# Phases rounded inside PSUM by matrix products, and new instruction orders for all engines of a two-layer spectral kernel

## The chip, the cores and the metric

The kernel runs on one core of a Trainium2 chip. The metric is device time in microseconds (us) of one execution. Five engines work side by side, each through its own queue in order: TensorE (PE, with its weight loads as PEld), VectorE (DVE), ScalarE (ACT), GpSimd (POOL) and SyncE (SP), which issues nearly all DMAs.

## The reference

Two kinds of layer alternate, A, B, A, B, each behind a layer norm and added to its input. A is a spectral filter (a 2-D FFT over 2048 rows and 512 channels, a product with weights, the way back); B is a diagonal state-space convolution (S4D): its kernel K of 2048 taps for each of the 512 channels is a sum over 128 complex powers, and the convolution runs through an FFT of length 4096.

```python
def _A_ref(x, w_r, w_i):
    X = rfft2(x, axes=(-2, -1)) * (w_r + 1j * w_i)
    return irfft2(X, s=(S, D), axes=(-2, -1))

def _B_ref(u, log_A_real, A_imag, C_real, C_imag, log_dt, D_skip):
    dt = jnp.exp(log_dt)
    A = -jnp.exp(log_A_real) + 1j * A_imag
    C = (C_real + 1j * C_imag) * dt[:, None]
    P = jnp.exp((A * dt[:, None])[:, :, None] * pos[None, None, :])
    K = 2.0 * jnp.einsum("dn,dnl->dl", C, P).real
    y = irfft(rfft(u_t, L2) * rfft(K, L2)[None], L2)[:, :, :L]
    return y.transpose(0, 2, 1) + u * D_skip[None, None, :]

x = x + _A_ref(_layernorm(x), A_w_r, A_w_i)
x = x + _B_ref(_layernorm(x), ...)
x = x + _A_ref(_layernorm(x), A_w_r, A_w_i)
x = x + _B_ref(_layernorm(x), ...)
```

Both B layers have the same K, which is made once.

## The kernel before

**FFTs as matrix products.** All transforms are products on TensorE in float32. A product of 128 output rows is issued as two products that take one half of the array's columns each (`halves`, L330), or as a list of products that lie side by side in the array (`side_by_side`, L336). Most take 128 rows of the array and 64 columns. The rows step of layer B (`p<-t,w` in the first, `p<-t,x` in the second B layer) takes 64 rows and 64 columns, four products at a time.

**K's time values.** `kernel_time` makes K in 32 units of 16 channels' states. For a unit, `grow` makes three tiles of magnitudes (`mag`): products of the constants `kb` with the states `th` in bfloat16, then exponentials on ScalarE. Each unit has two *turns*. `bend` makes the phases of a turn, counted in whole turns of the circle, in a PSUM tile `pk` by 4 products of 256 columns; VectorE rounds them to the nearest whole number by adding and subtracting 1.5 x 2^23 (`MAGIC`), into the bfloat16 tile `kw` (L864); two products of 512 columns with a negative identity `ni` subtract `kw` from `pk` again. What is left lies within half a turn. `sine` (an absolute value and a sine) and `cosine` run on ScalarE, `terms` multiplies both with the magnitudes on VectorE (L886, L888), `total` sums over the states on TensorE (`pv<-qp`, L899), ScalarE copies the sums to `stage` (L907), and a DMA takes them to the array `kt` in HBM. `kernel_freq` reads `kt` back and transforms it; layer B multiplies with the result (`kf`).

**What runs beside what.** K's 64 turns are interleaved with the first layer A and the beginning of the first layer B, since they need nothing of x. The last turn has to be done before the last block of K can be transformed.

**What sets the order.** After the program is built, `take_turns` lays the instructions of every engine in the order of the table `TURNS`: one string of places for each engine, found by a search outside the kernel. `ROOMS` says in the same way which buffer of a pool each tile takes, and `WARM` how many constant products are put ahead of which tile: `ps` issues them on a tile `warm` of ones into the PSUM tile that the next product overwrites. Nobody reads them; they keep TensorE from standing still.

## Time and profile before

| | us |
|---|---|
| median of 3 runs | 716.46 |
| lowest and highest | 710.45, 718.14 |
| span of the profiled execution | 713.4 |
| busy: PE, DVE, ACT, POOL | 626.0, 601.9, 438.2, 357.3 |
| products of the constant tile `warm`, part of PE's | 73.8 |
| mean granted TensorE clock | 0.973 |

The profile gives the profiled execution by its span, from the first to the last instruction; its own time beside that is not given apart, and the runs' median lies 3.1 us above the span. Busy times of one engine are unions: products that run side by side in the array count once. A float32 product leaves two records in the trace, a bfloat16 product one. Times in what follows are counted from the span's start.

### The profile page before, as it was taken

The numbers are of one execution on the slowest core, as the hardware profiler recorded it, in microseconds if no ns is written. First come the engines' busy times: TensorE is split into PE (matmuls) and PEld (weight loads), VectorE is DVE, ScalarE is ACT, GpSimd is POOL, SyncE is SP. The second block draws the span as 40 slices with busy tenths as digits, with TensorE's granted clock in tenths as the row PEclk, the third lists the DMA queues.
The fourth block names the chain that finished last, engine by engine and source line by source line (L and its number), as shares of the span: only waits on it lengthen the run. The fifth ranks groups of instructions, "written<-read, shape, count | busy, mean of one in ns | idle before, by whom it ended". The sixth has DMA issues, their size and how long they took to land. (4 is left out here: it accounts for less than half of the span.)

```text
span 713.4 us, 23503 instructions
## 1 busy us (share of the span) xinstructions
PE 626.0 (88%) x9580; PEld 491.3 (69%) x9580; DVE 601.9 (84%) x1348; ACT 438.2 (61%) x946; POOL 357.3 (50%) x565
## 2 busy tenths in 40 slices
PE   4459989989996999889999997984989899999996
PEld 3237867878674867667858876774877766577876
DVE  4998497998999799969999676869588699799993
ACT  3558999997664796778868524333767427333322
POOL 1533528672852704543196356452056484286870
PEclk9779999999999999999999999997999999999999
DMA  8602611613558350455544689222123103335514
GB/s 282 229 0 89 210 48 47 122 62 43 167 133 245 107 138 32 65 128 94 163 62 136 195 198 246 80 106 75 61 77 89 46 2 104 125 103 149 156 34 111
DMA packets 137355, 81.32 MB, mean 114 GB/s; under 512 B 70976, under 2 KB 116928, under 8 KB 136352
## 3 DMA queue, kind: packets, MB, share of 16 engines
q1 hardware_dynamic: 136992, 79.30, 40.1%
q8 instruction: 76, 1.25, 0.7%
q0 software_dynamic: 256, 0.52, 0.4%
q14 instruction: 31, 0.25, 0.1%
HBM read 54.90 MB, written 25.43 MB: 113 GB/s over the span
## 5 line engine op out<-in xcount | busy, mean ns | idle before, releaser
L1003 POOL TENSOR_TENSOR u<-wb,wb 64x512 f32<-64x512 f32 x90 | 123.2, 1373 | 66.0 <-DVE wb L991 60.9
L336 PE MATMUL p<-z,mb 128*64 128x512 f32 (+2 forms) x480 | 108.0, 517 | 1.7 <-DVE wb L991 1.3
L899 PE MATMUL pv<-qp 128*64 128x128 f32 x1024 | 81.6, 279 | 5.0 <-ACT stage L907 4.2
L991 DVE TENSOR_TENSOR wb<-p,kk 128x512 f32<-128x512 f32 x128 | 81.5, 676 | 4.3 <-POOL u L1003 2.3
L336 PEld LDWEIGHTS p<-mb,u 128*64 128x64 f32 x2048 | 73.1, 138 | 13.1 <-issue 6.7
L336 PE MATMUL p<-mb,u 128*64 128x64 f32 x2048 | 74.3, 223 | 4.4 <-issue 2.0
L663 ACT COPY z<-p 128x512 f32<-128x512 f32 x96 | 52.4, 595 | 41.8 <-PE p L336 31.6
L669 DVE STREAM_TRANSPOSE z<-z 128x512 f32<-128x512 f32 x96 | 59.3, 675 | 19.8 <-ACT z L663 19.7
L899 PEld LDWEIGHTS pv<-qp 128*64 128x64 f32 x1024 | 64.4, 139 | 15.8 <-ACT stage L907 6.9
L1113 POOL TENSOR_SCALAR w<-w,norms 128x128 f32<-128x128 f32 x64 | 34.7, 554 | 67.7 <-DMA w<-h 29.8
L547 POOL TENSOR_TENSOR w<-w,w 64x257 f32<-64x257 f32 x48 | 34.7, 724 | 66.8 <-DVE w L542 45.3
L1015 ACT COPY u<-p 128x512 f32<-128x512 f32 x64 | 35.9, 590 | 48.7 <-PE p L336 45.3
L330 PE MATMUL p<-w,w 128*64 128x256 f32 x256 | 38.2, 438 | 27.8 <-DVE w L463 11.6
L330 PE MATMUL pk<-kb,th 96*64 96x256 bf16 (+1 forms) x384 | 56.5, 312 | 1.5 <-DVE qp L888 1.1
L542 DVE TENSOR_TENSOR w<-wt,p 128x514 f32<-128x514 f32 x64 | 42.7, 688 | 17.1 <-PE p L336 9.6
L864 DVE TENSOR_SCALAR kw<-pk 128x512 bf16<-128x512 f32 x64 | 42.9, 680 | 16.5 <-PE pk L330 16.1
L330 PE MATMUL p<-warm 128*64 128x128 f32 x612 | 49.2, 284 | 3.2 <-DVE half L1139 1.1
L336 PE MATMUL p<-t,w 64*64 64x128 f32 x1024 | 42.1, 280 | 10.2 <-DMA w<-kt 3.5
L336 PEld LDWEIGHTS p<-z,mb 128*64 128x64 f32 x480 | 39.7, 137 | 16.1 <-issue 7.9
L330 PEld LDWEIGHTS p<-w,w 128*64 128x64 f32 x256 | 24.7, 156 | 36.3 <-DVE w L463 12.7
L336 PE MATMUL p<-w,ca 128*64 128x257 f32 x256 | 45.0, 385 | 4.1 <-ACT w L526 1.5
L832 ACT ACTIVATE kf<-pk 128x512 f32<-128x512 f32 x64 | 38.8, 606 | 15.4 <-PE pk L330 13.8
(179 smaller groups left out, 1617.1 us busy)
## 6 DMA issues: line engine op xcount, KB each, us to landing
wt<-in_w SPq DMA_DIRECT2D x32, 257.0 KB, 2.7
kf<-kk SPq DMA_DIRECT2D x32, 256.0 KB, 3.3
kk<-kf SPq DMA_DIRECT2D x32, 256.0 KB, 2.7
u<-in_x SPq DMA_DIRECT2D x16, 256.0 KB, 6.8
hr<-in_x SPq DMA_DIRECT2D x16, 256.0 KB, 3.9
kt<-stage SPq DMA_DIRECT2D x32, 128.0 KB, 5.2
h<-hr SPq DMA_DIRECT2D x16, 256.0 KB, 3.0
w<-kt SPq DMA_DIRECT2D x32, 128.0 KB, 3.1
```

What stands on the lines that cost most here:

```text
L330: self.nc.tensor.matmul(out[64 * r:64 * r + 64], weights[:, 64 * r:64 * r + 64], data, **k)
L336: last = self.nc.tensor.matmul(out, weights, data, start=not more, stop=True, skip_group_check=True).ins
L542: nc.vector.tensor_mul(m[pl], W, px[:, None, :].to_broadcast([128, 2, 257]))
L547: e[0].tensor_sub(Y[0:64, v], m[0][hs, 0], m[1][hs, 1])
L663: nc.scalar.copy(tiles["z"][:, :, :, b, m:m + 2].rearrange("p u j m r -> p (u j) (m r)"), ps[b].rearrange("p u j m r -> p (u j) (m r)"))
L669: nc.vector.transpose(tiles["zt"][:, u:u + 8].rearrange("p u j d -> p (u j d)"), tiles["z"][:, u:u + 8].rearrange("p u j b m r -> p (u j b ...
L832: nc.scalar.activation(*a, **k)
L864: nc.vector.tensor_scalar(whole, p, MAGIC, -MAGIC, op0=ALU.add, op1=ALU.add)
L899: nc.tensor.matmul(p[64 * t:64 * t + 64, g], QP[:, c, 2, d:d + 2].rearrange("p s a -> p (s a)"), QP[:, c, 0:2, d:d + 2].rearrange("p k s b ...
L991: nc.vector.tensor_mul(split(m[c, pl], "du", [32, 16]), by_channel(p), split(k[c], "du", [32, 16]))
L1003: self.added = e[0].tensor_sub(y[0:64], v[0, 0], v[1, 1]), e[1].tensor_add(y[64:128], v[0, 1], v[1, 0])
L1015: nc.scalar.copy(V[:, :, j, :, d:d + 8].rearrange("p n q d -> p q n d"), p.rearrange("p (q n) d -> p q n d", q=2))
```

## The change

Three edits go together.

The rounding moves to TensorE. `bend` now adds 1.5 x 2^23 to `pk` by a product of a bfloat16 tile `big`, which holds that number everywhere, with a weight tile that has a single row of ones (the first half of `ni`), and subtracts it by a second one with a row of minus ones; the sum in PSUM is then the rounded phase. Four more products of 256 columns subtract the phases from it again, with the negative constants LQ and LP at the end of `kb`. The sign of what is left turns over, so the sine's scale does too. The tile `kw` goes.

All orders (`TURNS`) and buffers (`ROOMS`) are new; `phase` lays out the rooms of its pools before any is used, and some tiles of a pool change place. By the change's own words the search counted the drain between products of 128 and of 64 rows.

`WARM` shrinks from 93 entries with 231 constant products (each of two halves) to 5 entries with 19.

```diff
-    out["ni"] = -np.eye(128)
-    out["kb"] = kb.reshape(96, 2560)
+    first = np.zeros((128, 2, 128))
+    first[0, 0], first[0, 1] = 1, -1
+    out["ni"] = first.reshape(128, 256)
+    out["kb"] = np.concatenate([kb, -kb[:, :, :512], -kb[:, :, 1536:2048]], 2).reshape(96, 3584)
...
+            for tag, v in tags.items():
+                if not isinstance(v, str):
+                    for k in range(v[1]):
+                        room = f"{tag}{k}" if v[1] > 1 else tag
+                        pool.tile([128, v[0] // 4], F32, tag=room, bufs=1, name=f"{name}_{room}")
...
-        self.kb = self.sb("kb", [2560], dt=BF, rows=96)
-        self.ni = self.sb("ni", [128], dt=BF)
+        self.kb = self.sb("kb", [3584], dt=BF, rows=96)
+        self.ni = self.sb("ni", [256], dt=BF)
+        self.big = self.sb("big", [512], dt=BF)
+        self.nc.gpsimd.memset(self.big, MAGIC)
...
-        KQ, RM, RN, KP, RP = (KB[:, k:k + 512] for k in range(0, 2560, 512))
+        KQ, RM, RN, KP, RP, LQ, LP = (KB[:, k:k + 512] for k in range(0, 3584, 512))
...
-            whole = self.sb("kw", [512], dt=BF)
             p = self.ps("pk", [2, 256])
-            self.halves(p[:, 0], th[:, h, 0], KQ[:, e], start=True, stop=False, skip_group_check=True)
-            self.halves(p[:, 1], th[:, h, 1], KP[:, e], start=False, stop=False, skip_group_check=True)
+            a, b = th[:, h, 0], th[:, h, 1]
+            self.halves(p[:, 0], a, KQ[:, e], start=True, stop=False)
+            self.halves(p[:, 1], b, KP[:, e], start=False, stop=False)
+            p0, p1 = p[:, 0], p[:, 1]
             p = p.rearrange("p k d -> p (k d)")
-            nc.vector.tensor_scalar(whole, p, MAGIC, -MAGIC, op0=ALU.add, op1=ALU.add)
-            self.halves(p, self.ni, whole, start=False, stop=True, skip_group_check=True)
+            self.halves(p, self.ni[:, 0:128], self.big, start=False, stop=False)
+            self.halves(p, self.ni[:, 128:256], self.big, start=False, stop=False)
+            self.halves(p0, a, LQ[:, e], start=False, stop=False)
+            self.halves(p1, b, LP[:, e], start=False, stop=True)
...
-            ordered(p, p, ACT.Sin, scale=-TAU)
+            ordered(p, p, ACT.Sin, scale=TAU)
...
-                    net.phase("a", x=(32768, 1), ta=(8192, 1), ca=(6912, 1), u=(16384, 2), w=(2056, WA), wt=(2056, WT),
+                    net.phase("a", x=(32768, 1), u=(16384, 2), ta=(8192, 1), w=(2056, WA), ca=(6912, 1), wt=(2056, WT),
...
 TURNS = {
     "tensor": """
-0-17 23-24 18-19 25-28 20-21 32-39 22 29-31 40-65 67-70 76-79 66 80-81 71-72 82-83 73-75 85-88 94-95 84 89-92
...
-WARM = {22: 7, 35: 3, 55: 1, 104: 3, 116: 2, 120: 5, 123: 6, 146: 2, 158: 1, 160: 2,
...
+WARM = {39: 7, 59: 1, 77: 3, 1184: 7, 1527: 1}
```

What the tables do to the queues shows at three places.

TensorE, a turn's products in the stage of K, before: the negative identity `ni` is multiplied with the rounded tile `kw`, and the next turn's first products follow (`kb` with the states `th`; every bfloat16 product has a weight load ahead of it).

```order
L330 MATMUL p_148_838<-w_756,ca_745 64x257 x2
L330 MATMUL p_155_872<-ca_745,x_82 64x2x2x33 x2
L330 MATMUL p_155_872<-ca_745,x_82 64x2x64 x2
L330 LDWEIGHTS ni_89
L330 MATMUL pk_779<-kw_778,ni_89 64x512
L330 LDWEIGHTS ni_89
L330 MATMUL pk_779<-kw_778,ni_89 64x512
L330 LDWEIGHTS th_679
L330 MATMUL pk_798<-kb_88,th_679 64x256
```

The same engine and stage now: four products with `big` stand where VectorE's rounding was waited for, then come the subtracting products with `kb`; in between lie products of layer A, some of them one half at a time (`p_286`, `p_288`).

```order
L343 MATMUL p_286_1629<-w_1546,ca_761 64x257
L337 LDWEIGHTS ni_118
L337 MATMUL pk_1689<-big_119,ni_118 64x512
L337 LDWEIGHTS ni_118
L337 MATMUL pk_1689<-big_119,ni_118 64x512
...
L343 MATMUL p_288_1634<-w_1546,ca_761 64x257
L337 MATMUL p_279_1572<-ca_761,w_1481 64x128 x2
L343 MATMUL p_288_1634<-w_1546,ca_761 64x257
L337 MATMUL p_279_1572<-ca_761,w_1481 64x128 x2
L337 LDWEIGHTS th_1408
L337 MATMUL pk_1689<-kb_117,th_1408 64x256
```

No product of the turn waits for VectorE any more, and layer A's halves have moved apart.

VectorE at the first turns, before: the rounding (L864) stands in the queue between layer A's weighing (L542, L547) and the terms of a turn (L886, L888).

```order
L801 TENSOR_TENSOR val_248<-val_248,hp_944 128x1920
L864 TENSOR_SCALAR kw_778<-pk_779 128x512
L542 TENSOR_TENSOR w_836<-wt_763,p_146_829 128x514
L542 TENSOR_TENSOR w_841<-wt_763,p_148_838 128x514
L864 TENSOR_SCALAR kw_797<-pk_798 128x512
L547 TENSOR_TENSOR w_843<-w_836,w_841 64x257
L542 TENSOR_TENSOR w_896<-wt_826,p_158_891 128x514
L864 TENSOR_SCALAR kw_854<-pk_855 128x512
```

The same place now (L549 and L554 are the weighing, L898 and L900 the terms):

```order
L549 TENSOR_TENSOR w_861<-wt_779,p_147_858 128x514
L549 TENSOR_TENSOR w_856<-wt_779,p_145_853 128x514
L554 TENSOR_TENSOR w_863<-w_856,w_861 64x257
L549 TENSOR_TENSOR w_918<-wt_850,p_156_915 128x514
L549 TENSOR_TENSOR w_923<-wt_850,p_158_920 128x514
L898 SCALAR_TENSOR_TENSOR qp_830<-pk_817,mag_723 128x256
L898 SCALAR_TENSOR_TENSOR qp_807<-pk_794,mag_723 128x256
L900 TENSOR_TENSOR qp_807<-pk_794,mag_723 128x512
```

The weighing follows itself, and the terms of two turns come together.

TensorE at the seam between the second layer A and the last layer B, before: 64-row products (`t` with `x`) are cut by constant products (`warm`).

```order
L330 MATMUL p_1556_8493<-wv_8412,ta_8054 64x512 x2
L330 MATMUL p_1564_8519<-wv_8434,ta_8054 64x512 x2
L336 MATMUL p_1586_8598<-t_8052,x_8056 64x64x2
L330 MATMUL p_1587_8599<-warm_71 64x128 x6
L336 MATMUL p_1587_8599<-t_8052,x_8056 64x64x2 x2
L336 MATMUL p_1586_8598<-t_8052,x_8056 64x64x2 x3
```

The same place now: the same products are cut by products of layer A's last rows (`u` with `ca`, `wv` with `ta`).

```order
L337 MATMUL p_1487_8462<-ca_6824,u_7403 64x128 x3
L343 MATMUL p_1523_8576<-t_8052,x_8056 64x64x2
L343 MATMUL p_1524_8577<-t_8052,x_8056 64x64x2
...
L343 MATMUL p_1523_8576<-t_8052,x_8056 64x64x2
L343 MATMUL p_1524_8577<-t_8052,x_8056 64x64x2
L337 MATMUL p_1487_8462<-ca_6824,u_7403 64x128
L337 MATMUL p_1493_8485<-wv_8404,ta_8054 64x512 x2
L343 MATMUL p_1523_8576<-t_8052,x_8056 64x64x2
```

The constant products have left, and the 64-row products now have changes of another kind among them.

More of the change, by code (lines that the diff above doesn't have):

```diff
@@ new lines @@
+    "p.p1": "1303201321013102303212002331132013230322133020321303120013231020312103102212031210313221212113101201"
+        "230201020122",
+    "v.hp": "101010",
+    "k0.th": "0101010101010101",
+    "k.mag": "23013201023102310231023132012013",
+    "pk.pk": "0220112201201201021112210110210221002220102101202201120010210120002120221020120111120112021021210121"
+        "0110021021021200111021021012",
+    "a.wt": "0231031230312013",
+    "k.qp": "3024130243140231230214301240312440132401230142302342014242013420",
@@ new lines @@
+    "e.hr": "7210634572604312",
+    "f.z": "1010101010101011001010101",
+    "f.w": "6352145443120513604623130456546320154120536143604211526056132406514035461465320643251306402315436025"
+        "1643026514362056143016523410625431046251360543216035412035132612163035460132503463350240612045316203"
+        "5403614203543140625541365201462311051506243016235042",
+    "pm.p1": "1010010101101010100111001100101010011011011010010111001011011010010101010110",
+    "b.kk": "407651325031276451607324367354030465701325763106512676157210217601750465307143267510436035761245",
@@ L1493 @@
+    "pm.p2": "0100011010100101010110100101101011001010",
+    "b.u": "100101",
+    "pb.p2": "100212010221002101201010",
+    "wide.wb": "05231740357741264037316520314651",
+    "pb.p1": "01231212304102323104430231021332030",
+    "wide.xw": "3021",
+    "pc.p3": "0021110111211010212212211201201202120212012102102101211012221012011212001202120121201210220102212012"
+        "2101221202010",
     "folds.fa": "1010",
-    "folds.xf": "0101",
-    "pc.p1": "0101010101010101010101010101010101010101010110010101011001011001",
```

447 lines of the change are left out of this document (205 added, 242 removed), and 9 rows, old and new, of the table WARM.

## The prediction

> **What bounds the kernel now.** First the page's busy line, then the same sums cut at the stages: start (0 to 60 us), the stage in which the S4D kernel's time values are made beside layer A and the first rows of layer B (60 to 396), the rest of layer B (396 to 486), the second layer A (486 to 600), the last layer B. Columns of the windows: length, then busy us (instructions) of PE, PEld, DVE, ACT, POOL, the granted clock, DMA share, GB/s.
>
> ```profile
> PE 626.0 (88%) x9580; PEld 491.3 (69%) x9580; DVE 601.9 (84%) x1348; ACT 438.2 (61%) x946; POOL 357.3 (50%) x565
> ...
> 0.00:60.00 60.00, 30.73 (x218) 21.06 (x220) 49.60 (x133) 30.20 (x67) 21.60 (x45) 0.83 0.47 155
> 60.00:396.00 336.00, 311.21 (x4609) 245.70 (x4606) 300.90 (x659) 269.19 (x550) 172.37 (x298) 0.99 0.43 111
> 396.00:486.00 90.00, 80.04 (x1422) 64.97 (x1418) 64.83 (x145) 34.01 (x65) 48.83 (x55) 1.00 0.62 168
> 486.00:600.00 114.00, 99.90 (x1298) 78.93 (x1300) 92.02 (x243) 63.17 (x185) 51.41 (x119) 0.96 0.20 60
> 600.00:713.40 113.40, 104.16 (x2040) 80.61 (x2036) 94.54 (x171) 41.60 (x81) 63.07 (x48) 0.99 0.38 114
> ...
> 180.00:230.00 50.00, 44.37 (x520) 30.01 (x516) 49.90 (x130) 29.81 (x60) 29.90 (x53) 1.00 0.63 181
> ```
>
> In the long stage TensorE shows 311.2 of 336 us and VectorE 300.9; at 180 to 230 us VectorE has no idle time at all (49.90 of 50). But part of TensorE's time is filler: products of the constant tile `warm`, which nobody reads. The same stages for that tile alone (PE, PEld, DVE), and then the groups by form:
>
> ```profile
> 0.00:60.00 60.00, 5.14 (x44) 4.25 (x44) 0.22 (x1) 0.83 0.47 155
> 60.00:396.00 336.00, 49.12 (x620) 37.28 (x620) 0.00 (x0) 0.99 0.43 111
> 396.00:486.00 90.00, 8.92 (x124) 8.07 (x124) 0.00 (x0) 1.00 0.62 168
> 486.00:600.00 114.00, 4.46 (x60) 3.46 (x60) 0.00 (x0) 0.96 0.20 60
> 600.00:713.40 113.40, 6.19 (x76) 4.42 (x76) 0.00 (x0) 0.99 0.38 114
> ...
> sum 713.40, PE 73.83 PEld 57.48 DVE 0.22; mean PE 14.77 PEld 11.50 DVE 0.04
> ```
>
> ```profile
> L330 PE MATMUL pk<-kb,th 96*64 96x256 bf16 x256 | 31.1, 274 | 0.6 <-DVE qp L888 0.5
> L330 PE MATMUL pk<-kw,ni 128*64 128x512 bf16 x128 | 29.3, 382 | 2.4 <-DVE kw L864 2.2
> ...
> L864 DVE TENSOR_SCALAR kw<-pk 128x512 bf16<-128x512 f32 x64 | 42.9, 680 | 16.5 <-PE pk L330 16.1 <-PE p L336 0.2
> ...
> L330 PE MATMUL pk<-kb,th x384: 269/274/634, 70.7 to 379.8; 96*64 96x256 bf16 x128, 96*64 96x512 bf16 x64
> L864 DVE TENSOR_SCALAR kw<-pk x64: 650/681/693, 79.8 to 382.9; 128x512 bf16<-128x512 f32 x64
> ```
>
> (In a group: busy us, mean ns of one, idle time before them and what ended it; the last two rows give first and last start.) The turns run from 70.7 to 382.9 us.
>
> So TensorE's own work in the long stage is 311.2 - 49.1 = 262.1 us, and VectorE, with 300.9, is the engine with the most of it: today this stage is set by VectorE and by the way the two hand to each other. From 396 us on it is the other way: TensorE's work without filler is 284.1 - 19.6 = 264.5 us of 317.4, VectorE's 251.4, and no turn is rounded there.
>
> **The rounding, out of VectorE.** 64 TENSOR_SCALARs of 680 ns go, all in the long stage: VectorE falls from 300.9 to 258.0 us there. The 16.1 us in which it stood idle for a turn's products go too, as does the hop from TensorE to VectorE and back that ScalarE's sine waits for. What is late next on VectorE are the `terms` (L886, L888), which wait for ScalarE.
>
> **The rounding, into TensorE.** A turn had 4 products of 256 columns and 2 of 512; it gets 8 of 256 and 4 of 512, so 256 and 128 instructions more. By the busy time in the rows above that is 256 x 0.121 + 128 x 0.229 = 60.4 us. But busy time holds the pipeline's fill when a product stands alone. The timeline shows what a pair of halves costs in a stream (start to start):
>
> ```profile
> 103.10 0.39 PE L330 MATMUL pk<-kb,th 96*64 96x512 bf16 x2
> 103.32 0.61 PE L899 MATMUL pv<-qp 128*64 128x128 f32 x8
> ...
> 223.54 0.31 PE L330 MATMUL pk<-kb,th 96*64 96x256 bf16 x2
> 223.65 1.07 PE L899 MATMUL pv<-qp 128*64 128x128 f32 x16
> ```
>
> That is 0.22 us for a pair of 512 and 0.11 for a pair of 256: 128 x 0.11 + 64 x 0.22 = 28.2 us. The twelve products of a turn wait for nothing between them, which speaks for the stream; the order shows halves of other products put between them, which speaks for more. I take 40, nearer the stream.
>
> TensorE's work in the stage is then 262.1 + 40 = 302 us (290 to 322), above VectorE's 258.0 and ScalarE's 269.2: **the bound changes hands**. Today TensorE with its filler stands idle for 24.8 of 336 us, 7.4%. If the new bound is served as well, the stage lasts 302 / 0.926 = 326 us, **10 us less**; at the ends 290.3 / 0.926 = 313.5 (-22) and 322.5 / 0.926 = 348 (+12). In other words: the stage breaks even where the added products cost the 49.1 us that the filler took.
>
> **Filler outside that stage.** Of 924 records 76 remain. Most stood in waits and their going is worth nothing. At the seam to the last layer it cuts the 64-row products in two:
>
> ```profile
> 595.55 0.43 PE L336 MATMUL p<-t,x 64*64 64x128 f32 x2
> 595.91 0.66 PE L330 MATMUL p<-warm 128*64 128x128 f32 x8
> 596.50 1.10 PE L336 MATMUL p<-t,x 64*64 64x128 f32 x30
> ...
> 608.63 0.87 PE L336 MATMUL p<-t,x 64*64 64x128 f32 x10 [0.51 <-ACT z L663]
> ```
>
> Here TensorE is full, and the block from 595.91 to 596.50 delays 30 products by 0.6 us. The 76 records between 600 and 616 us take 6.2 us; I take half, **-3 us** (0 to -8 with the drains around them), since the copies of `z` on ScalarE hold some of these products anyway, as the last row shows.
>
> **Drains.** A change between 128 and 64 rows shows in the step from start to start:
>
> ```profile
> 234.22 0.39 PE L330 MATMUL p<-warm 128*64 128x128 f32 x4
> 234.54 0.34 PE L336 MATMUL p<-t,w 64*64 64x128 f32 x4
> ```
>
> Four records are two pairs, 0.11 us apart; the next product starts 0.32 us after the first of them, so 0.21 after the last: 0.1 us is the drain. Although the search is said to count it, the new order changes over more often: 78 groups of 64-row products for 46, 156 changes for 92, counted in the two orders. 64 x 0.1 = 6.4 us; some fall where TensorE would wait, so half, **+3 us** (0 to +6.4).
>
> **The clock.** Two waits and what followed them (first the wait in brackets, then the window after it):
>
> ```profile
> 230.23 0.51 PE L336 MATMUL p<-t,w 64*64 64x128 f32 x8 [2.39 <-DMA t<-in_t]
> 314.23 1.10 PE L336 MATMUL p<-t,w 64*64 64x128 f32 x30 [1.71 <-DMA w<-kt]
> 442.91 1.32 PE L336 MATMUL p<-t,w 64*64 64x128 f32 x40 [1.35 <-DMA w<-kt]
> ...
> 230.52:233.93 3.41, 3.41 (x48) 3.08 (x42) 3.41 (x13) 1.07 (x2) 1.76 (x2) 0.50 0.98 271
> 315.85:319.27 3.42, 3.42 (x34) 2.68 (x34) 0.00 (x0) 2.48 (x6) 3.23 (x5) 0.50 0.41 114
> ...
> 221.99 1.75 PE L330 MATMUL pk<-warm 128*64 128x128 f32 x28 [0.28 <-DVE qp L888]
> ```
>
> After waits of 2.39 and 1.71 us the clock fell to half for 3.4 us; at 1.35 us the stage's clock stays at 1.00. Each fall costs 3.4 x 0.5 = 1.7 us where TensorE is the bound. Without the filler at 221.99 there would be a gap of 1.8 us. But the long stage gets denser by 40 us of products, so I take as many falls as today: 0.
> The Trainium skill, TensorE: Matmul & The Clock Gate, section "Why this matters for your kernels", speaks of drops after idle gaps of some 3 us; the trace has one after 1.71, so by the rule the removed filler costs nothing and by the trace it can cost.
>
> **The rest.** ScalarE loads its tables 22 times for 24, with no bound on ScalarE: 0. The constants `kb` grow from 480 to 672 KB on POOL's queue at the start:
>
> ```profile
> kb<-in_kb POOLq DMA_DIRECT2D x1, 480.0 KB, 8.6
> ```
>
> They have landed after some 12 us by the same rate (an estimate from this row), and the first product that reads them stands at 70.7: 0. The orders of all five engines are new, so every other wait moves; I have no row for that and put it at 0 with the bounds below.
>
> **Sum.** 713.4 - 10 - 3 + 3 = **703 us**, against the profiled execution's span of 713.4; the median of the runs is 716.46, 3 us above it, and I leave that to the range.
>
> **Rivals.**
> - *A larger gain* (0.15). The turns stream at 28 us and the order fills half of TensorE's waits: 290.3 / 0.963 = 301.5 in the stage, -35; with the seam, 676. For it: VectorE loses 42.9 us and 16.1 us of waits. Against it: TensorE would be 96% busy over 336 us, which it is now only with filler that can go anywhere.
> - *Nothing to see* (0.20). The stage ends earlier, and what follows it waits for its own chain, rows to copies to transposes to pairs; 317 us with 53 us of TensorE idle or filler are not touched by the rounding. Then the ten us shrink to two or three: 711.
> - *The clock* (0.07). Five more falls at gaps that the filler closed (as at 221.99), 5 x 1.7 = 8.5: 711.5. By the skill's rule this has no chance; by the rows at 230.23 and 314.23 a small one.
> - *Slower: TensorE is overfull* (0.13). The rounding costs its busy price, 60 us for the 49 of filler, because halves put singly between others leave one half of the columns idle; +12 in the stage, +6.4 drains, no gain at the seam: 713.4 + 18.4 = 732. It decides from 49 us of added products upward. For it: in the new order two successive full-row products go to the same half of the columns 339 times, before 242 (counted in the orders). Against it: filler was in the way of products too.
>
> **How the numbers follow.** The forecast (694 to 712) has 0.45, most of it below 709.3, which is 1% under the median; 1% is about what a measurement of this kernel can tell from no change (the three runs spread over 1.1%). Faster by over 1%: 0.15 and 0.43 of the forecast, 0.58. Within 1%: 0.02 + 0.20 + 0.07 = 0.29. Slower: 0.13. The range of 8 in 10 runs from 684, which cuts off about half of the larger gain, to 727, which cuts off most of the overfull case.
>
> **What would show it.** Right: no `kw` on VectorE; VectorE's busy time near 559, TensorE's near 626 - 68 + 40 = 598 (848 records of filler at 0.080 us go); the last turn near 370 to 375 us; in the long stage waits of VectorE for `pk` products through ScalarE, hardly any of TensorE. Wrong: the price, if the 256 new products of 512 columns show well over 0.15 us of busy time each; the drains, if 64-row products wait longer than 0.1 us at a change; the clock, if more than four stretches show half of it. The prediction as a whole falls if stages without turns, after 400 us, change by more than the long one: then it is the new order that counts and not the rounding.

## The result: 711.4 us for 717.7, and the profile after

The changed kernel takes 711.44 us (median of 20 runs, 708.71 to 715.21), the kernel before beside it 717.65 (20 runs, 710.45 to 719.83): a ratio of 0.993, 95% interval 0.992 to 0.995. The forecast was 703. The sign is right and the time lies in the range, but the gain is a third of the one forecast, 0.7% for 2%. The profiled execution's span is 709.2 us, 4.2 less than before, where 10.4 were forecast.

First the busy line of the changed kernel's page.

```profile
PE 640.5 (90%) x9116; PEld 468.1 (66%) x9116; DVE 576.6 (81%) x1284; ACT 435.0 (61%) x944; POOL 356.2 (50%) x566
```

TensorE was to fall from 626 to 598 us: 848 records of constant products left, and the rounding's products came. It rose. To see where, both executions are cut at the same marks: 60 us, the last product of the long stage (`pv`), the first product of the second layer A (`kk,xf`), the first of the last layer (`t,x`), the end. Columns as in the prediction: length, then busy us (instructions) of PE, PEld, DVE, ACT, POOL, the granted clock, DMA share, GB/s. Before:

```profile
60.00:412.50 352.50, 327.71 (x4837) 259.25 (x4832) 309.31 (x687) 277.64 (x566) 177.57 (x310) 0.99 0.45 117
412.50:492.00 79.50, 63.54 (x1199) 51.46 (x1193) 62.41 (x143) 26.60 (x54) 43.62 (x43) 0.97 0.57 149
492.00:595.50 103.50, 95.39 (x1232) 75.78 (x1232) 82.57 (x203) 59.03 (x175) 48.30 (x113) 0.98 0.19 55
595.50:713.40 117.90, 108.66 (x2106) 83.72 (x2104) 97.99 (x184) 44.68 (x88) 66.18 (x54) 0.99 0.38 112
```

After:

```profile
60.00:390.80 330.80, 320.45 (x4497) 242.44 (x4493) 276.61 (x607) 270.07 (x550) 171.84 (x295) 1.00 0.46 115
390.80:478.10 87.30, 73.96 (x1165) 49.11 (x1162) 65.48 (x147) 31.25 (x63) 48.94 (x52) 0.97 0.63 168
478.10:578.30 100.20, 94.18 (x1179) 76.86 (x1179) 83.83 (x200) 55.77 (x169) 47.94 (x114) 0.97 0.18 52
578.30:709.20 130.90, 120.07 (x2030) 79.18 (x2028) 99.78 (x190) 47.58 (x93) 64.77 (x54) 0.96 0.34 104
```

The long stage is 21.7 us shorter, but the next one takes 7.8 of that back, so at the first product of the second layer A the new kernel is 13.9 us ahead (492.0 to 478.1); at the end of that layer it is 17.2 (595.5 to 578.3). Then **the last layer gives 13 us back**: 130.9 us for 117.9, with TensorE busy for 11.4 us more although 76 fewer records run in it. No rounding happens there.

The groups by form show that the same products take up more of TensorE's busy time, though one by one they are hardly longer (busy us, mean ns of one, idle before). Before, then after:

```profile
L336 PE MATMUL p<-z,mb 128*64 128x512 f32 x288 | 101.0, 597 | 1.7 <-DVE wb L991 1.3 <-DVE z L669 0.3
L899 PE MATMUL pv<-qp 128*64 128x128 f32 x1024 | 81.6, 279 | 5.0 <-ACT stage L907 4.2 <-DVE qp L888 0.7
```

```profile
L343 PE MATMUL p<-z,mb 128*64 128x512 f32 x288 | 114.7, 608 | 1.8 <-DVE z L676 1.7
L911 PE MATMUL pv<-qp 128*64 128x128 f32 x1024 | 99.7, 276 | 1.7 <-DVE norms L389 0.7 <-ACT stage L919 0.6 <-DVE qp L900 0.3
L337 PE MATMUL pk<-kb,th 96*64 96x256 bf16 x512 | 63.1, 274 | 2.1 <-DVE qp L900 1.8 <-ACT mag L841 0.2
L337 PE MATMUL pk<-big,ni 128*64 128x512 bf16 x256 | 46.2, 380 | 0.0
```

Busy time of a group is a union: two products side by side in the two halves of the columns count once. The same 288 records of 0.6 us each (`z,mb`) cover 13.7 us more: they no longer lie side by side. The same holds for `pv<-qp` in the long stage, 18.1 us more; what each of the two is worth in time, the experiments tell apart. The timeline of the last layer shows what has come between them (start, length, records in a row; a float32 product leaves two records):

```profile
635.27 0.59 PE L343 MATMUL p<-z,mb 128*64 128x512 f32 x1
635.28 0.22 PE L343 MATMUL p<-mb,u 128*64 128x64 f32 x1
635.33 0.96 PE L343 MATMUL p<-z,mb 128*64 128x32 f32 x3
636.23 0.44 PE L343 MATMUL p<-t,x 64*64 64x128 f32 x4
636.59 1.14 PE L343 MATMUL p<-z,mb 128*64 128x512 f32 x6
```

A `z,mb` product of 512 columns starts at 635.27 on one half. Its partner on the other half is issued in two pieces, 32 and 480 columns. The 32 run beside it (635.33, two records of some 0.03 us; the third record in that row is the second one of the 512); the 480 come behind the 64-row products `t,x`. Those start only when the long product is through, so the other half stands still from about 635.40 to 636.23, some 0.83 us. The change comes between the two halves of one pair, **26 times in the new order and never in the old one**.

From the records, each put on its half by its place in the order, I sum how long one half had been free before the other at the changes from 128 to 64 rows: before 1.3 us, after 41.3. These are estimates: a float32 record of 512 columns is taken to stream for 0.43 us (the two records of the long product above start at 635.27 and 635.71), the others in proportion. By the same lengths, in none of the 46 and 78 changes to 64 rows of the two traces does the first record start sooner than 0.09 us after the later half has streamed its last one: the change waits for both halves every time. In the whole span one half runs alone for 70 us before and for 135 after.

### The profile page after: what moved, and what is told of

It reads as the page before. It is cut to its first block, busy times and chain, and to the rows that moved or that the text cites. A ratio compares the mean times of both kernels' runs of the same rounds, so it can differ in the third digit from the quotient of the medians.

```text
span 709.2 us, 22438 instructions
## 1 busy us (share of the span) xinstructions
PE 640.5 (90%) x9116; PEld 468.1 (66%) x9116; DVE 576.6 (81%) x1284; ACT 435.0 (61%) x944; POOL 356.2 (50%) x566
## 5 line engine op out<-in xcount | busy, mean ns | idle before, releaser
L343 PE MATMUL p<-z,mb 128*64 128x512 f32 (+2 forms) x480 | 138.9, 524 | 1.8 <-DVE z L676 1.7
L911 PE MATMUL pv<-qp 128*64 128x128 f32 x1024 | 99.7, 276 | 1.7 <-DVE norms L389 0.7
L337 PE MATMUL pk<-kb,th 96*64 96x256 bf16 (+1 forms) x640 | 90.6, 296 | 3.3 <-DVE qp L900 1.8
L670 ACT COPY z<-p 128x512 f32<-128x512 f32 x96 | 52.3, 590 | 59.0 <-PE p L343 47.4
L911 PEld LDWEIGHTS pv<-qp 128*64 128x64 f32 x1024 | 73.0, 136 | 17.2 <-issue 7.2
L343 PEld LDWEIGHTS p<-mb,u 128*64 128x64 f32 x2048 | 69.4, 140 | 13.9 <-issue 10.5
L337 PEld LDWEIGHTS <-th 96*64 96x64 bf16 x640 | 49.1, 109 | 23.1 <-issue 10.2
L549 DVE TENSOR_TENSOR w<-wt,p 128x514 f32<-128x514 f32 x64 | 42.4, 687 | 24.1 <-PE p L343 17.2
L343 PEld LDWEIGHTS p<-z,mb 128*64 128x64 f32 x480 | 40.9, 138 | 29.8 <-issue 18.7
L337 PE MATMUL p<-ca,u 128*64 128x128 f32 (+2 forms) x512 | 56.2, 301 | 0.4 <-ACT u L570 0.3
L337 PE MATMUL p<-ca,w 128*64 128x128 f32 x512 | 52.6, 276 | 3.2 <-DVE w L556 1.0
L337 PE MATMUL p<-w,w 128*64 128x256 f32 x256 | 35.4, 408 | 21.5 <-ACT w L465 16.9
L343 PE MATMUL p<-w,ca 128*64 128x257 f32 x256 | 52.5, 386 | 2.4 <-ACT w L533 1.2
L337 PEld LDWEIGHTS p<-ca,u 128*64 128x64 f32 x512 | 43.2, 136 | 11.9 <-issue 6.4
L343 PEld LDWEIGHTS p<-t,w 64*64 64x64 f32 x1024 | 32.7, 132 | 26.7 <-issue 14.9
```

What stands on the lines that cost most here:

```text
L337: self.nc.tensor.matmul(out[64 * r:64 * r + 64], weights[:, 64 * r:64 * r + 64], data, **k)
L343: last = self.nc.tensor.matmul(out, weights, data, start=not more, stop=True, skip_group_check=True).ins
L549: nc.vector.tensor_mul(m[pl], W, px[:, None, :].to_broadcast([128, 2, 257]))
L670: nc.scalar.copy(tiles["z"][:, :, :, b, m:m + 2].rearrange("p u j m r -> p (u j) (m r)"), ps[b].rearrange("p u j m r -> p (u j) (m r)"))
L911: nc.tensor.matmul(p[64 * t:64 * t + 64, g], QP[:, c, 2, d:d + 2].rearrange("p s a -> p (s a)"), QP[:, c, 0:2, d:d + 2].rearrange("p k s b ...
```

## Experiments

Each kernel ran beside the kernel before on one chip; ratios are to it. "Pairs" are the products of the two halves of one output tile, with the 32 and 480 columns of `z,mb` as one side; the last two columns are sums over the span, estimated from the records as above (a_oldround's were not summed). They depend on how short gaps are counted (a stricter count gives 81 and 173 us for the 70 and 135), the order of the runs hardly does. Not all rows are from the same chip, so a difference of a few us between two of them is given by the ratios too.

| run | median us | ratio, 95% interval | changes of row mode | one half alone, us | neither half, us |
|---|---|---|---|---|---|
| before | 716 to 719 | 1 | 92 | 70 | 132 |
| changed kernel | 711.4 | 0.993 (0.992-0.995) | 156 | 135 | 116 |
| a_joined | 696.3 | 0.974 (0.971-0.977) | 146 | 106 | 116 |
| a_joined_tail | 700.3 | 0.977 (0.973-0.981) | 152 | 120 | 112 |
| b_split | 723.8 | 1.010 (1.006-1.013) | 92 | 83 | 135 |
| a_paired | 694.0 | 0.968 (0.964-0.971) | 146 | 73 | 126 |
| a_whole | 714.6 | 0.999 (0.996-1.002) | 80 | 109 | 131 |
| a_cut | 715.6 | 0.997 (0.994-1.000) | 224 | 114 | 127 |
| a_near | 704.6 | 0.981 (0.977-0.984) | 98 | 71 | 138 |
| a_near4 | 696.1 | 0.969 (0.965-0.973) | 118 | 71 | 130 |
| a_paired_seam | 694.6 | 0.967 (0.964-0.970) | 148 | 75 | 129 |
| b_nofiller | 713.0 | 0.995 (0.993-0.998) | 76 | 70 | 168 |
| b_round_nofiller | 736.6 | 1.029 (1.025-1.034) | 76 | 68 | 155 |
| b_round | 745.4 | 1.041 (1.036-1.045) | 92 | 67 | 130 |
| a_oldround | 733.8 | 1.026 (1.019-1.032) | 150 | | |
| a_round2 | 712.2 | 0.994 (0.991-0.998) | 146 | 104 | 104 |

### Are the cut pairs the loss?

**a_joined.** The edit is in TensorE's order alone. At one place, as the program's rows (the `t` rows are the 64-row products):

```
 p_630 <- z,mb  64x512 x2
-p_635 <- z,mb  64x512
-p_635 <- z,mb  64x32
 p_646, p_647 <- t,w  ...
 p_631 <- z,mb  64x512 x2
+p_635 <- z,mb  64x512
+p_635 <- z,mb  64x32
 p_635 <- z,mb  64x480
```

> The changed kernel with 49 of its 5006 products at another place in TensorE's order, nothing else: in 26 places of the new order a change from 128 to 64 rows (or back) stands between the products of the two halves of one pair, so that one half of TensorE's columns runs alone for up to 0.86 us; here the first of each such pair is put right before its partner. Changes 156 to 146. Theory (halves out of step: in the trace of the changed kernel one half waits for the other just before changes of row mode for 41 us of half columns in all, before the change for 1.3 us, and the last layer is 13 us longer): 4 to 14 us faster than the changed kernel, last layer (from its first 64-row product to the end) 131 to about 120 us, TensorE busy 640 to about 620. Rival A (TensorE overfull by the rounding's products): same within 2 us, last layer as it was. Rival B (clock or missing filler at the seam to the last layer): same within 2 us.

696.29 us, 15 less than the changed kernel. The windows, at the same marks as above:

```profile
60.00:387.10 327.10, 315.54 (x4495) 240.38 (x4491) 276.32 (x607) 269.74 (x550) 173.16 (x295) 0.99 0.45 115
387.10:474.80 87.70, 72.73 (x1170) 48.76 (x1165) 65.27 (x149) 31.58 (x64) 48.98 (x52) 0.98 0.64 170
474.80:573.50 98.70, 92.88 (x1176) 75.49 (x1176) 83.79 (x200) 55.64 (x169) 48.13 (x114) 0.99 0.18 53
573.50:694.60 121.10, 111.14 (x2030) 79.12 (x2028) 98.30 (x191) 47.52 (x93) 66.03 (x54) 0.96 0.36 113
```

The last layer is down from 130.9 to 121.1 us, the same 2030 records in 8.9 us less of busy time; TensorE in all from 640.5 to 624.7. `z,mb` is back from 114.7 to 104.3 us at the same length of a record:

```profile
L343 PE MATMUL p<-z,mb 128*64 128x512 f32 x288 | 104.3, 604 | 1.4 <-DVE z L676 1.0 <-ACT kk L966 0.2
```

A place in the last layer, as it looks with the pair uncut:

```profile
615.74 1.08 PE L343 MATMUL p<-z,mb 128*64 128x512 f32 x4
616.65 0.31 PE L337 MATMUL p<-u,mb 128*64 128x32 f32 x4
616.89 1.19 PE L343 MATMUL p<-t,x 64*64 64x128 f32 x32
```

Both halves of a pair, four records, are through in 0.91 us; above, a single half held up the other for 0.83. The sum at the changes falls from 41.3 to 9.9 us. Rivals A and B, which expected no change, are out.

**a_joined_tail.** The same edit for the 13 cut pairs of the last layer only.

> The changed kernel with only the 13 cut pairs of the last layer joined; the 13 of the stages before it stay cut. Theory: the last layer takes 121 us as in the joined run and not 131, all before it stays as in the changed kernel, so 8 to 11 us faster than that: 700 to 704. Rival (the joined run was faster since the earlier stages ended sooner, and the last layer only followed): last layer 127 us or more, 706 to 711.

700.33 us, 11 less. By the windows the stages before stay as they were (the last layer begins at 578.0 us, in the changed kernel at 578.3), while the last takes 121.2:

```profile
578.00:699.20 121.20, 111.18 (x2029) 78.73 (x2028) 98.23 (x190) 47.43 (x93) 65.98 (x54) 0.97 0.36 113
```

**b_split.** The reverse on the kernel before: in 11 places one half's product and its partner come to stand on two sides of 64-row products (three of the pairs, at the layer's start, are the last products of layer A).

```
-p_x <- z,mb  (second half)
 t,x  64-row products of a call
+p_x <- z,mb  (second half)
```

> The reverse: the kernel before, with one half's product of 11 pairs of the last layer put behind the 64-row products that follow the pair, nothing else. Changes 92 as before; by stream time one half then runs alone for 4.4 us more. Theory: last layer 118 to 121 to 126 us, in all 3 to 8 us slower than before. Rival (cut pairs don't matter by themselves): within 2 us of before.

723.75 us, 7.4 slower; the last layer takes 124.3 us for 117.9 (the profiled execution, the longest of its runs, is 4.4 us behind already when that layer begins, where nothing was moved):

```profile
599.90:724.20 124.30, 114.66 (x2107) 86.36 (x2106) 97.73 (x184) 44.68 (x88) 65.83 (x54) 0.99 0.36 106
```

The sum at the changes rises from 1.3 to 8.6 us. (The 4.4 us of the expectation counted one of the two records of a float32 product; the trace shows 7.3.) Taking cut pairs away and putting them in both move the time as the theory says, in the same stage.

### Is it the change of mode, or any pair out of step?

**a_paired.** On top of a_joined, the halves of some 140 pairs that stood apart with only 128-row products between them are put next to each other.

> As the run with joined pairs, and in addition 142 pairs whose halves had other products between them, but no change of row mode (48 of 257 columns, 23 of 512 with 32 and 480, 30 of 128 and others): the earlier half is put right before the later. Work and number of changes (146) are those of the joined run. Theory, widened (whatever puts the halves out of step costs, not the change itself): one half running alone falls from 106 us in the joined run towards 80, and the kernel is 4 to 12 us faster than the joined run, 684 to 692. Rival (only a change of row mode makes a half wait for the other; elsewhere the queue fills the gap): within 2 us of the joined run. Rival (the halves of those pairs stood apart because the second was not ready): 3 us or more slower, with waits of TensorE for ScalarE or VectorE in their place.

694.03 us, 2.3 less than a_joined by the medians and some 4.6 by the ratios: between the first rival (2) and the widened theory (4 to 12). One half alone falls from 106 to 73 us, while the time in which neither half runs rises from 116 to 126. The rows that had grown shrink again, and TensorE's busy time falls from 624.7 to 616.2 us:

```profile
L911 PE MATMUL pv<-qp 128*64 128x128 f32 x1024 | 84.2, 276 | 3.6 <-ACT stage L919 1.9 <-DVE qp L900 0.9 <-DVE norms L389 0.6
L337 PE MATMUL pk<-kb,th 96*64 96x256 bf16 x512 | 51.3, 275 | 3.3 <-DVE qp L900 2.6 <-ACT mag L841 0.4
L337 PE MATMUL pk<-big,ni 128*64 128x512 bf16 x256 | 40.7, 383 | 0.0
```

In a_joined `pv<-qp` still had the 99.7 us of the changed kernel. So the 18 us that it had gained in busy time came from halves that stood apart without a change of mode, and they were worth few us of time at most: there the queue had filled the gap, or a wait took its place. The cut pairs, with 10.4 us in `z,mb`, were worth 15.

### What does a change cost by itself?

**a_whole.** On top of a_joined, the 64-row products of a call are kept together where their last stood, for 20 of the 22 calls cut by other products.

> As the run with joined pairs, and in addition 64-row products of one call kept together at the place of their last (20 of 22 calls that were cut): changes 156 to 80, pairs uncut. Theory: the number of changes costs about 0.1 us each, so 66 fewer than in the run with joined pairs give up to 6 us of TensorE, of which at most half is on the path; within 3 us of the joined run, since the first of a call's products come later and what they feed with them. A rival, that each change costs far more than 0.1 us (a drain for every one, 0.3 us): 10 us or more faster than the joined run.

714.6 us: 18 **slower** than a_joined with 66 fewer changes. Neither theory had this. **a_cut** goes the other way: 39 whole pairs are moved from ahead of a call into its middle.

> The run with joined pairs, with 39 whole pairs (both halves, next to each other) moved from just before a call's 64-row products into the middle of them: changes 146 to 224, no half put out of step by stream time. It measures the change by itself. Theory: what is left between the rows at a change is the drain, 20.8 us for 146 changes in the joined run's trace, 0.14 us each, so 78 more cost 11 us of TensorE; between half of that (the forecast's share) and all of it shows: 5 to 11 us slower than the joined run, 701 to 707. Rival (a change without halves out of step is free): 695 to 698. Rival (a change costs far more than the gap that the trace shows): over 715.

715.62 us, 19 slower by the medians (17 by the ratios). The gap between the last record before a change and the first one after it, summed, grew from 20.8 to 29.6 us, 0.11 us for each of the 78; the sum of halves out of step at 128 to 64 only from 9.9 to 11.4. About half of the loss is thus the gaps themselves; the rest isn't explained by the records, and the moved pairs' readers come later too. To tell a price of 0.25 us from a side effect, **a_near** and **a_near4** start from a_paired and join calls that only a few products cut (24 calls cut by up to 8; 14 by up to 4).

> The run with all pairs next to each other, with 24 calls' 64-row products, cut by up to 8 products of 128 rows, put together again by passing those few products by the shorter piece of the call: changes 146 to 98, pairs uncut. Price of a change of its own, 0.25 us by the cut run (19 us for 78): 12 us faster than the run with all pairs, 680 to 685. Price by the gap in the trace, 0.11 to 0.14 us: 5 to 7 us faster, 687 to 689. Rival (what stood between filled waits, as the run with whole calls, 66 changes fewer and 18 us slower, suggests): 694 or more.

> The same for the 14 calls cut by at most 4 products: changes 146 to 118. By 0.25 us each 7 us faster than the run with all pairs, 685 to 689; by the gap 3 to 4, 690 to 691; if what stood between filled waits, 694 or more.

704.62 and 696.06 us, with 48 and 28 fewer changes than a_paired. The first is 10.6 us slower (9.3 by the ratios); the second, with 2.0 and 0.9, can't be told from a_paired. The waits of TensorE show a part of the reason (engine, what for: us in all, times, longest); first a_paired, then a_near:

```profile
PE p L343 <- ACT z L670: 3.1, 5, 1.2
```

```profile
PE p L343 <- ACT z L670: 9.6, 11, 1.5
```

The products that cut a call stood where 64-row products wait for the copy of the tile before (`z`, L670): without them TensorE waits 6.5 us more. In a_whole the same wait grew from a_joined's 3.3 us to 7.8, 4.5 of the 18. In both the stretch at half the clock at the seam grew as well, from 6.8 to 13.7 us. The rest of the two losses isn't explained. The price of 0.25 us for a change left out is ruled out in both runs, that of 0.12 in a_near; the third case of the expectations holds. What a change costs with everything else held still isn't settled: the gap that it leaves in the trace is 0.11 to 0.14 us, and a_cut's whole loss, side effects and all, is 0.22 to 0.25 for each.

### The constant products

**b_nofiller.** `WARM = {22: 7, 35: 3, 55: 1}` in the kernel before.

> The kernel before with 440 of its 462 constant products left out (those of the start stay), all else and every order as before. Theory: they stood in TensorE's waits for VectorE, so little changes: 0 to 4 us faster, VectorE as busy as before, long stage within 4 us of before. Rival B (without them the clock falls to half in the waits): more stretches at half clock than the 5 before, 5 to 15 us slower.

712.99 us, 3.4 less by the medians (ratio 0.993 to 0.998): of rival B only the clock is there, with 8 stretches at half for 5 (one in the last 2 us of the span before left out), and they cost less than the products gave back. The long stage, the second layer A and the last layer:

```profile
60.00:410.40 350.40, 307.42 (x4216) 225.91 (x4212) 309.78 (x687) 276.75 (x566) 178.05 (x310) 0.98 0.45 118
491.00:591.10 100.10, 91.40 (x1177) 73.33 (x1178) 80.53 (x198) 57.03 (x169) 48.28 (x113) 0.98 0.20 57
591.10:712.90 121.80, 108.07 (x2018) 82.23 (x2016) 98.97 (x184) 44.44 (x88) 65.85 (x54) 0.94 0.37 108
```

The second layer A gains 3.4 us and the last layer loses 3.9 (before: 103.5 and 117.9). And TensorE's busy time falls by far less than the constants' own: in the long stage from 327.7 to 307.4 us, in all from 626.0 to 596.2, 29.8 us for 880 records of which the kernel before had 73.8 us in 924. An explanation that fits, but that no run tests: the busy time of the products around a constant one overlapped with its own, and counts in full without it.

**a_paired_seam** puts 23 constants back at the seam (one more than its expectation says):

```diff
-WARM = {39: 7, 59: 1, 77: 3, 1184: 7, 1527: 1}
+WARM = {39: 7, 59: 1, 77: 3, 1184: 7, 1527: 4, 1493: 2, 1501: 2, 1509: 2, 1525: 4, 1528: 4, 1547: 4, 1532: 2}
```

> The run with all pairs next to each other, with 22 constant products (44 with both halves) put back at eight places where TensorE waits at the seam to the last layer, about as many as the kernel before has there. In the run with all pairs the clock fell to half from 586.4 to 593.2 us, after TensorE had been busy for 6.3 of 10 us; in the kernel before, with constants there, it did not fall at the seam. Without its constants the kernel before took 3.9 us longer in its last layer. Theory (the missing constants cost the half-clock stretch): no half clock there, 2 to 4 us faster than the run with all pairs, 690 to 692. Rival (the constants only stand in the way, or the wait comes from elsewhere): same within 1.5 us, or slower.

694.55 us, the same as a_paired. The clock does what the theory says, first without, then with the constants:

```profile
580.00:590.00 10.00, 6.33 (x92) 3.91 (x96) 6.24 (x27) 6.99 (x14) 0.07 (x1) 0.82 0.72 262
590.00:600.00 10.00, 10.00 (x83) 4.01 (x76) 9.31 (x17) 2.15 (x4) 3.40 (x3) 0.84 0.19 55
```

```profile
580.00:590.00 10.00, 8.43 (x148) 6.11 (x150) 6.85 (x28) 7.88 (x15) 1.56 (x3) 1.00 0.51 181
590.00:600.00 10.00, 8.63 (x126) 4.89 (x120) 8.01 (x14) 2.19 (x5) 1.03 (x1) 1.00 0.25 90
```

No half clock there, and no gain: at the seam TensorE waits for `z` copies either way.

### What is the rounding's move worth?

**b_round_nofiller** and **b_round** move the rounding alone: old orders, the turn's eight products where the second product with the negative unit matrix stood, without and with the constants.

```diff
-            nc.vector.tensor_scalar(whole, p, MAGIC, -MAGIC, op0=ALU.add, op1=ALU.add)
-            self.halves(p, self.ni, whole, start=False, stop=True, skip_group_check=True)
+            self.halves(p, self.ni[:, 0:128], self.big, start=False, stop=False)
+            self.halves(p, self.ni[:, 128:256], self.big, start=False, stop=False)
+            self.halves(p0, a, LQ[:, e], start=False, stop=False)
+            self.halves(p1, b, LP[:, e], start=False, stop=True)
```

> The kernel before with the rounding moved to TensorE (eight products where the second product with the negative unit matrix stood, VectorE's 64 roundings gone) and 440 of 462 constant products left out, but in the old orders and old buffers: what it lacks of the change is the search's new orders. Theory (rounding and missing filler bring the long stage's gain, the new orders lose it again at the row mode changes): long stage 12 to 16 us shorter than before, last layer at 116 to 120 us as before, 700 to 706 us in all, so faster than the changed kernel by 5 to 10 us. Rival A (rounding makes TensorE overfull): no faster than before, 716 to 725. Rival C (new orders are what brings the gain of the long stage): 714 to 720.

> The kernel before with the rounding moved to TensorE in the old orders and all 462 constant products kept. The run of the same without the constant products took 736.6 us, 20 more than before, and its long stage 14 more. Theory A (TensorE in the long stage is full by the rounding's 49 us, whatever stands in the gaps): the constant products (some 40 us in that stage) come on top where no gap is left for them: 737 to 750, long stage longer still. Theory B (in the old order the rounding's eight products wait in TensorE's queue at places made for two; the constant products only fill those waits and keep the clock): 728 to 737.

736.64 and 745.41 us: 20 and 29 **slower** than before. My theory for the first was 700 to 706, the worst miss of these runs. The long stages, from 60 us to the last `pv`:

```profile
60.00:426.90 366.90, 325.78 (x4605) 250.31 (x4602) 280.87 (x624) 278.30 (x567) 175.19 (x310) 0.97 0.43 113
```

```profile
60.00:442.90 382.90, 355.19 (x5231) 287.26 (x5226) 278.99 (x627) 280.20 (x569) 172.95 (x310) 0.97 0.41 108
```

VectorE is busy for 28 and 30 us less than before, and TensorE for 89 and 93% of the stage where the changed kernel has 97%: the stage gets longer with no engine full. The constants come on top, as theory A of the second run said. **a_oldround** does the opposite to a_joined: the rounding back on VectorE under the new orders (with three buffers for the rounded values). Its subtracting products use the weights with one row of minus ones, so every row loses the first row's whole turns and not its own, and what is left need not lie within half a turn. The instructions are those of a rounding on VectorE and last as long as in the kernel before (681 ns for a rounding, 680 before; 595 for a sine, 604 before).

> The run with joined pairs (new orders, few constant products), but with the rounding back on VectorE: 64 roundings there, put into VectorE's new order where the products before them end, and one pair of products with the negative unit matrix in place of the eight, some 2 us after them as in the kernel before (median there 2.5 us). By the joined run's windows TensorE is busy 316 of the 327 us from 60 to 387, VectorE 276; the rounding's price is 46 us of TensorE or 43 us of VectorE, so TensorE would have 269 and VectorE 319. Theory (the rounding's move changes the bound of the long stage from VectorE to TensorE, and takes some 10 us off): VectorE binds again, stage 319 / 0.93 = 343 us, in all 705 to 715. Rival (the orders bring all of the gain, the rounding's place none): 690 to 700.

733.81 us, 37 slower, above both theories. VectorE is busy for 315 us, near the 319 foreseen, but in 361.7 us and not 343:

```profile
60.00:421.70 361.70, 311.10 (x4115) 220.53 (x4111) 315.39 (x672) 270.94 (x550) 173.09 (x295) 0.98 0.41 105
```

ScalarE's wait for a turn's phases says where some of it goes; before, in a_joined, in b_round and in a_oldround:

```profile
ACT kf L832 <- PE pk L330: 13.8, 12, 2.8
```

```profile
ACT kf L841 <- PE pk L337: 8.5, 9, 4.1
```

```profile
ACT kf L837 <- PE pk L332: 22.3, 21, 3.3
```

```profile
ACT kf L841 <- PE pk L337: 21.2, 14, 4.4
```

With each rounding in the order made for it, the wait is short; with either in the other's order it grows by 9 to 13 us. As placed in these runs, rounding and order can't be priced apart: both swaps cost, and only the two together gain. An order searched anew for the rounding on VectorE was not run, so how much of the gain the rounding's place is needed for stays open.

**a_round2** doubles the four products with `big` in a_joined.

> The run with joined pairs, with the four products that add and take away the large constant made twice (256 products of 512 columns more, the rounded values stay as they are). Theory (TensorE binds the long stage, 316 of 327 us busy): nearly the whole of what they add comes on top, 27 us by stream time of two halves (256 x 213 ns / 2) to 45 us by busy time, so 721 to 741. Rival (TensorE still has slack there, another engine's chain binds): up to 12 us more, 696 to 708.

712.18 us, 15.9 slower, between the two theories. The products' row in a_joined and here, and the long stage here:

```profile
L337 PE MATMUL pk<-big,ni 128*64 128x512 bf16 x256 | 45.3, 380 | 0.0
```

```profile
L337 PE MATMUL pk<-big,ni 128*64 128x512 bf16 x512 | 73.3, 379 | 0.0
```

```profile
60.00:400.60 340.60, 334.48 (x4745) 258.98 (x4744) 278.58 (x607) 270.21 (x549) 172.70 (x295) 1.00 0.44 111
```

28.0 us of these products' busy time were added and the stage grew by 13.5 (it ended at 387.1, now at 400.6). So **half** of what TensorE gets there shows: it is in part the bound, not wholly.

## Why the prediction was wrong, by its own steps

- **Drains: +3 forecast, some +15 in the runs. This is the step that failed.** The prediction took 0.1 us for each of 64 more changes from a place where the two halves ended together, and counted half of that. (Beside the old order without its constants, which has 76 changes by b_nofiller, they are 80 more.) The gap that a change leaves is indeed that small: by the sum 0.14 us in both kernels, 12.8 us for 92 and 21.5 for 156. But a change also waits for the later of the two halves, and the new order cuts 26 pairs. That wait had no term in the sum. Joining the pairs gives 15 us back, and the last layer's 13 pairs alone give 11. The Trainium skill, TensorEngine Tiling (Array Packing), section "Key Properties", says that a change of the tiling mode drains TensorE while tiles of one mode run independently of each other. The trace agrees with both: one half runs on by itself after 635.27, and the change waits for it while the other stands still for some 0.83 us.
- **The long stage: -10 forecast, -13.9 measured** to the first product of the second layer A (-21.7 in the stage itself and 7.8 back in the next). Its parts missed in opposite directions. The added products cost 48.9 us by busy time (63.1 + 46.2 less 31.1 + 29.3), not 40, and 0.18 us for each new product of 512 columns, over the 0.15 that the prediction named as a sign against its price. In a_paired the same rows make 31.6 (51.3 + 40.7 less 31.1 + 29.3): the price hangs on whether the halves stand together. TensorE's "own work" of 262.1 us was too low: taking the constants out lowers its busy time in the stage by 20 us (b_nofiller) and not by the 49.1 that their own rows show. And TensorE is busy for 97% of the stage (320.45 of 330.80) and not for 92.6: the sentence "if the new bound is served as well" took the old order's waits for granted. The last turn begins at 372.5, as foreseen (370 to 375). That the bound moves to TensorE is half right, by a_round2.
- **What made the stage faster** was put down to VectorE's 42.9 us and 16.1 us of waits. The runs don't bear that out as a cause by itself: with them gone and the old orders kept the kernel is 20 to 29 us slower. The prediction put "every other wait moves" at 0 with no row for it.
- **Busy times.** TensorE 640.5 us for 598. The prediction took 68 us off for the 848 records, at 0.080 each; b_nofiller's 29.8 for 880 make 0.034 each, so some 29. That is most of the 42.5 us. VectorE 576.6 for 559: `qp<-qp,mag` went from 706 to 753 ns each, others likewise.
- **The seam: -3 forecast.** It priced constants between 600 and 616 us, in the last layer. There b_nofiller loses 3.9 us; what it gains at one place, 3.4 us, lies ahead of that in the second layer A, where the changed kernel is 3.3 us shorter too. That the size agrees is luck. The 3.2 us by which a_joined's last layer is still longer than before (121.1 for 117.9) look like b_nofiller's 3.9, but the constants put back in a_paired_seam don't bring them; where they come from is open.
- **The clock: 0 forecast**, right in the sum (mean 0.973 before, 0.980 after). The stretches at half after the waits at 230 and 314 us are gone and two are new, at 459.5 and at the seam (592.7 to 602.9 us); the one at the seam costs nothing that shows, by a_paired_seam.
- **The rivals.** "Overfull" named the mechanism, halves put singly, and took its sign from the order's 339 successive products into one half for 242. But a_joined has 341 of them and is 15 us faster, and a_paired has 247 and gains a few us more: that count isn't what costs. The rival looked for the loss in the long stage, at the price of the rounding; it came at the row changes, most of it in the last layer. "Nothing to see" gave 711, the time measured, but by another way: the early stages did gain more than forecast, and the last layer lost it again. That the time fell on 711 and into the range is luck, two misses of opposite sign. The clause that would fell the prediction, later stages that change by more than the long one, does not apply as a whole (+7.8, -3.3 and +13.0 against -21.7), but the last layer alone undoes 13 of the 17.2 us gained before it.

The fastest order here is a_paired (a_paired_seam and a_near4 can't be told from it): 694.0 us, 3.2% under the kernel before. It differs from the changed kernel only in where the products of these pairs stand in TensorE's order.

## What to carry to other kernels

In these traces a change of row mode is a barrier for both halves of the array. Keep the halves of a pair on the same side of it, and count not the changes but how far the halves are apart when one comes. Halves that stand apart without such a change raise TensorE's busy time and cost little (2 to 5 us in a_paired), so busy time alone doesn't tell the two apart. Fewer changes are no aim by themselves: what stands between 64-row products may fill their wait. An order and the placing of an operation that were found together may not be priced one by one; here, an edit tried in the other's order said little about the edit.

## What the runs showed of the hardware

The clock fell without a long gap. In the changed kernel, at the seam, with waits in brackets, then the window after:

```profile
589.67 0.44 PE L337 MATMUL p<-warm 128*64 128x128 f32 x4 [0.67 <-ACT z L670]
590.56 0.43 PE L343 MATMUL p<-t,x 64*64 64x128 f32 x2 [0.45 <-ACT x L634]
591.82 2.54 PE L343 MATMUL p<-t,x 64*64 64x128 f32 x30 [0.84 <-ACT z L670]
```

```profile
592.70:602.90 10.20, 8.26 (x51) 3.17 (x50) 4.86 (x8) 1.56 (x3) 0.00 (x0) 0.50 0.35 133
```

No wait in these rows is longer than 0.84 us, but from 589.0 to 591.8 TensorE was busy for 0.87 of 2.8 us, and the clock went to half for 10.2 us. In a_paired_seam, with constants between them, longer waits left it at full:

```profile
586.39 1.09 PE L337 MATMUL p<-warm 128*64 128x128 f32 x16 [0.69 <-ACT z L670]
588.37 1.09 PE L337 MATMUL p<-warm 128*64 128x128 f32 x16 [0.89 <-ACT z L670]
...
591.72 0.55 PE L337 MATMUL p<-warm 128*64 128x128 f32 x6 [1.22 <-ACT z L670]
```

The prediction's pair of waits, 1.35 us without a fall and 1.71 with one, thus sets no threshold for a single gap; how busy TensorE is over some microseconds fits these rows better, though no run here separates the two.
